# Exponentials left in the scores' PSUM bank, masks built on the chip, first weight blocks converted in halves

## The chip, the cores and the metric

The kernel runs on one core of one Trainium2 chip, in one launch. Its time is the device time in microseconds (us). Each measurement below is the median of several runs, with the lowest and the highest beside it. A separate profiled execution gives the trace: every instruction of the engines TensorE (PE for its products, PEld for its weight loads), VectorE (DVE), ScalarE (ACT), GpSimd (POOL) and SyncE (SP, which only issues DMAs here).

## The reference, cut to what matters

Sliding-window attention feeds a three-matrix mixture layer, and that a SiLU layer:

```
attention: q, k, v of (4, 8, 576, 64); S = q k^T / 8; position i sees j with 0 <= i - j < 64
           x = softmax(masked S) v, heads side by side: (2304, 512)
layer 1:   h = (x w1) * (x w2);  x2 = (h w3) w_out     w1, w2: 512 x 1024, w3: 1024 x 1024, w_out: 1024 x 512
layer 2:   h = x2 w_in;  out = (h * sigmoid(h)) w_out  w_in: 512 x 2048, w_out: 2048 x 512
```

The weights reach the chip as 64-bit floating point words, and the chip makes 32-bit numbers of them.

## The kernel before, in words

**Converting a weight.** Weights come in chunks of 128 x 512 numbers, that is 128 x 1024 32-bit words, 512 KB each, by a DMA of SP's queue. A chunk takes five steps: ACT scales the high words (L125, tile cv_b) and rounds the low words (L128, cv_r), DVE shifts (L138, cv_z) and puts the sign in (L141), and POOL adds the two (L145). The chunks of w1 and w2 then get a rounded half and a rest (L153, L157). `line` is the list of chunks; `loads_to` issues their DMAs, `steps_to` and `fill` drop their steps in between other work.

**Attention.** The 2304 positions are 18 units of 128, with 4 pairs of heads each: 72 groups g. A group has two heads, and each of its steps works for both. The scores (PE, L329 for the first 17 groups, L333 and L337 for the rest) go to the PSUM tile s, 128 x 2 x 192, of which there is one buffer: 128 queries against 192 keys. DVE adds a mask to each head, scales, writes the result to the SBUF tile sm and takes the extreme of each row into nm (L344, two instructions; the masks are constants, tile consts, loaded by three DMAs of SP). ACT raises each head to its exponential in place in sm, with the row's sum in es (L355: each of the two is an ACTIVATE and a READ of the accumulator). DVE adds the parts of the sum (L363), takes the reciprocal (L365) and multiplies (L367, "the normalise", which reads and writes sm). PE transposes the result (L377, three instructions, tile t), ACT and DVE take it out of PSUM (L383, or L387 to L392), and PE multiplies it with the values (L404 to L412, tile o). ACT and DVE take o out (L419 to L422), and POOL finishes it (L423, xr). sm has two buffers, used in turn.

**Stage W, 0 to about 93 us.** Since nothing lies between the products with w3 and with w_out, the chip first computes wp = w3 w_out: 16 steps s of 4 products (L582, 128x512 each), with one chunk of w3 each, and in the first 8 steps one of w_out too. Chunks of w1 and w2 follow among them at the steps that W12_BY names. `half(h)` runs half a group: the even half issues for g, in this order on PE, the scores of g, the values of g-2 and the transposes of g-1, and on ACT the exponentials of g; the odd half issues on DVE the normalise of g, and the preparations of later groups (L297 to L321). 28 halves stand in this stage. Before it, "spin" products on a constant tile (L525) keep PE at work.

**Stage A, 93 to about 401 us.** Six blocks of 384 positions. Each has 24 units of products, one group of the attention to every two: 16 "ab" units (L618: x w1 and x w2, multiplied elementwise over L632, L634 and split by L85) and 8 "x" units (L648, with wp; L601 takes the result out, L602 stores it). The other groups run here.

**Layer 2, to the end.** Products hx, hy (L828) and o (L882), with sums of weights and activations made by ACT, DVE and POOL.

**What sets the order.** Each engine runs its instructions in the order in which the program issues them, and waits at each for the semaphores of what it needs. The order is written out, by the loops above; no scheduler changes it.

## Time and profile before

| | us |
|---|---|
| median of 3 runs (lowest, highest) | 841.4 (841.26, 842.33) |
| the profiled execution | 841.24 |
| its span, from the first to the last instruction | 839.5 |
| busy: PE / PEld / DVE / ACT / POOL | 827.4 / 745.9 / 615.3 / 561.2 / 529.7 |

The span is what the trace shows; 1.74 us of the profiled execution lie outside of it. PE's granted clock is 1.000 of full speed over the whole span. In the rows further down, a row of a timeline tells when an instruction started, how long it took, its engine, line and operation, the tile written and the tile read, and in brackets how long the engine was idle before it and what released it. A row of the groups tells the busy time of all instructions of one line and shape and the mean of one in ns.

### The profile page before, as it was taken

How to read it: one execution, taken by the hardware profiler on the slowest of the kernel's cores; microseconds unless marked ns; L12 is line 12 of the kernel's file. 1: busy time of each engine (PE TensorE's matmuls, PEld its weight loads, DVE VectorE, ACT ScalarE, POOL GpSimd, SP SyncE). 2: the span in 40 equal slices, each digit the busy share in tenths (PEclk: the TensorE clock that was granted, in tenths of full speed). 3: DMA queues.
4: the chain of work that ended last, by engine and by line, in shares of the span. 5: the costliest groups of instructions: out<-in, count | busy, mean ns of one | idle time of the engine just before them, and what ended most of it. 6: DMA issues, size and time to landing. Idle time of an engine off the chain costs nothing.

```text
span 839.5 us, 14173 instructions
## 1 busy us (share of the span) xinstructions
PE 827.4 (99%) x4418; PEld 745.9 (89%) x4418; DVE 615.3 (73%) x1424; ACT 561.2 (67%) x1390; POOL 529.7 (63%) x588
## 2 busy tenths in 40 slices
PE   7999999999999999999999999999999999999998
PEld 3555799999999999999999988888888888988986
DVE  7889877688888888888368698998644567644544
ACT  6889778898898898898556566556543446443433
POOL 5768666677777677677565577876454456454441
PEclk9999999999999999999999999999999999999999
DMA  9998234444544544543433522301301201201002
GB/s 320 330 321 279 72 107 128 149 127 133 167 150 142 169 156 145 170 157 103 155 134 120 194 76 76 125 26 51 102 26 56 95 26 64 88 25 51 1 1 75
DMA packets 54682, 102.66 MB, mean 122 GB/s; under 512 B 5200, under 2 KB 32592, under 8 KB 54608
## 3 DMA queue, kind: packets, MB, share of 16 engines
q1 hardware_dynamic: 51008, 96.91, 35.5%
q10 hardware_dynamic: 3600, 4.85, 1.6%
q8 instruction: 35, 0.57, 0.3%
q14 instruction: 39, 0.32, 0.1%
HBM read 88.11 MB, written 13.63 MB: 121 GB/s over the span
## 4 chain that ended last, share of the span: by engine, by line
PE 69%; POOL 8%; ACT 6%; issue 4%; DVE 1%; ACTq 0%; POOLq 0%; DVEq 0%
PE o L882 24%; PE ab L618 14%; PE hy L828 12%; PE hx L828 9%; PE x L648 6%; POOL klo L303 2%; POOL vhl L321 1%; ACT sm L355 1%; PE t L377 1%; POOL xr L423 1%; ACT qkhi L297 1%; POOL p L88 1%; POOL cv_b L189 1%; PE o L411 1%; PE s L333 1%
## 5 line engine op out<-in xcount | busy, mean ns | idle before, releaser
L882 PE MATMUL o<-hl,gp 128*128 128x512 f32 x504 | 133.3, 394 | 0.0
L618 PE MATMUL ab<-xa,hl 128*128 128x384 f32 x576 | 119.0, 341 | 0.0
L828 PE MATMUL hy<-xop,j 128*128 128x384 f32 x576 | 115.9, 335 | 0.0
L618 PE MATMUL ab<-xb,hl 128*128 128x384 f32 x570 | 115.2, 334 | 0.0
L88 POOL TENSOR_TENSOR gp<-tmp,gp 128x384 fp32r<-128x384 f32 x56 | 64.1, 1145 | 77.5 <-ACT gp L85 75.9
L828 PEld LDWEIGHTS hy<-xop,j 128*128 128x128 f32 x576 | 102.6, 188 | 9.0 <-DVE tmp L722 1.0
L882 PEld LDWEIGHTS o<-hl,gp 128*128 128x128 f32 x504 | 93.1, 188 | 13.1
L618 PEld LDWEIGHTS ab<-xb,hl 128*128 128x128 f32 x570 | 100.3, 188 | 0.0
L618 PEld LDWEIGHTS ab<-xa,hl 128*128 128x128 f32 x576 | 99.1, 188 | 0.0
L844 ACT ACTIVATE tmp<-hx 128x384 f32<-128x384 f32 x48 | 23.6, 492 | 111.5 <-DVE hx L722 67.8
L722 DVE TENSOR_TENSOR tmp<-hy,tmp 128x384 f32<-128x384 f32 x96 | 53.2, 554 | 56.1 <-PE hy L828 51.5
L828 PE MATMUL hx<-xop,j 128*128 128x384 f32 x432 | 86.6, 335 | 0.0
L882 PE MATMUL o<-hl,gq 128*128 128x512 f32 x324 | 85.9, 393 | 0.0
L88 POOL TENSOR_TENSOR gq<-tmp,gq 128x384 fp32r<-128x384 f32 x36 | 39.0, 1084 | 74.3 <-ACT gq L85 74.3
L828 PEld LDWEIGHTS hx<-xop,j 128*128 128x128 f32 x432 | 76.8, 188 | 4.1
L423 POOL TENSOR_TENSOR xr<-ot 128x128 f32<-128x128 f32 x55 | 32.7, 594 | 73.7 <-DVE ot L422 65.5
L303 POOL TENSOR_TENSOR klo<-qk,qkhi 64x192 fp32r<-64x192 f32 x110 | 67.2, 611 | 7.6 <-ACT qkhi L297 2.7
L882 PEld LDWEIGHTS o<-hl,gq 128*128 128x128 f32 x324 | 60.3, 188 | 11.2
L648 PE MATMUL x<-p,wp 128*128 128x384 f32 x360 | 69.6, 339 | 0.0
L355 ACT ACTIVATE sm<-sm,nm 128x192 f32<-128x192 f32 x144 | 64.5, 450 | 3.9 <-DVE nm L344 2.5
L648 PEld LDWEIGHTS x<-p,wp 128*128 128x128 f32 x360 | 61.9, 188 | 0.0
L145 POOL TENSOR_TENSOR cv_b<-cv_b,cv_r 128x512 int32<-128x512 int32 x32 | 48.6, 1520 | 18.8 <-DVE cv_b L141 9.4
(146 smaller groups left out, 1896.7 us busy)
## 6 DMA issues: line engine op xcount, KB each, us to landing
qk<-in_qkv SPq DMA_DIRECT2D x55, 384.0 KB, 3.1
words<-in_w_out SPq DMA_DIRECT2D x24, 512.0 KB, 5.4
r<-w_in SPq DMA_DIRECT2D x22, 512.0 KB, 3.4
words<-in_w3t SPq DMA_DIRECT2D x16, 512.0 KB, 6.5
words<-in_w SPq DMA_DIRECT2D x16, 512.0 KB, 6.2
xe<-in_w_in SPq DMA_DIRECT2D x16, 512.0 KB, 4.8
v<-in_qkv SPq DMA_DIRECT2D x55, 96.0 KB, 2.7
x2d<-x2s ACTq DMA_DIRECT2D x24, 192.0 KB, 1.9
```

The source lines that it names most:

```text
L88: (nc.vector if eng_lo == "dve" else nc.gpsimd).tensor_tensor(out=lo, in0=src, in1=f32(hi), op=ALU.subtract)
L145: nc.gpsimd.tensor_tensor(out=x, in0=b, in1=self.r, op=ALU.add)
L189: nc.gpsimd.tensor_tensor(out=self.b, in0=self.b, in1=self.r, op=ALU.add)
L303: nc.gpsimd.tensor_tensor(out=k_lo[g % 2][hs, h * 192 : h * 192 + 192], in0=t[hs, n], in1=f32(hi[hs, n]), op=ALU.subtract)
L355: nc.scalar.activation(out=x, in_=x, func=AF.Exp, scale=-1.0, bias=nm[:, h : h + 1], accum_out=sums_of[g % 2][:, h, 0:1])
L423: nc.gpsimd.tensor_tensor(out=xr[:, c, r : r + 128], in0=t[:, 0:128], in1=t[:, 128:256], op=ALU.add)
L618: nc.tensor.matmul(acc, lhsT=w[:, l, fs], rhs=x[k // 2][:, k % 2, r, :], start=(k == 0 and n == 0), stop=(k == 3 and n == 2),)
L648: nc.tensor.matmul(acc, lhsT=wp[f][:, l, o * 128 : (o + 1) * 128], rhs=p[f][:, r, :], start=(f == 0 and n == 0), stop=(f == 7 and n == 2),)
L722: eng.tensor_tensor(out=out, in0=a, in1=b, op=op)
L828: nc.tensor.matmul(bank[name], lhsT=w[:, l, at + kt], rhs=x[:, kt, r, :], start=(fresh and kt == 0 and n == 0), stop=(kt == 1 and n == 2), ...
L844: nc.scalar.activation(out=sg, in_=src, func=AF.Sigmoid)
L882: nc.tensor.matmul(oacc[t], lhsT=g[:, l, cols], rhs=weights["out", 2 * p + i][:, r, :], start=(p == 0 and i == 0 and n == 0), stop=(p == P ...
```

## The change

It has five parts. (1) The exponentials write to the scores' PSUM tile instead of sm, and the normalise reads that tile and writes sm. (2) The even half of a group issues on PE the values of g-2, the transposes of g-1 and then the scores of g. (3) The masks and the identity are built in consts by memsets on DVE and selections on POOL, the mask of the rarest kind by a copy and two memsets on POOL at step 4; the three mask DMAs are gone, and the zeroing of kq moves to DVE and that of klo to step 4. (4) The first chunks, 0, 1 and 3, are converted in halves of 256 columns, the first step issues its four products in a row, and SP's first loads have another order. (5) The second chunk of w1 is due at step 4 instead of 3.

On PE in stage W, around the scores of group 8: o6 are the values of group 6, t7 the transposes of group 7, s8 the scores of group 8, accw the products of w3 with w_out. Before:

```order
L329 MATMUL s8_608<-kq0_81 128x384
L404 MATMUL o6_618<-pw0_96,vp0_83 128x128
L405 MATMUL o6_618<-pw0_96,vp0_83 128x128
L406 MATMUL o6_618<-pw0_96,vp0_83 128x64
L377 MATMUL t7_623<-consts_69,sm1_78 128x128 x3
L582 MATMUL accw1_2_589<-wo_94,q_95 128x512
L582 MATMUL accw1_3_590<-wo_94,q_95 128x512
L582 MATMUL accw1_0_587<-wo_94,q_95 128x512
L582 MATMUL accw1_1_588<-wo_94,q_95 128x512
```

With the change:

```order
L451 MATMUL o6_647<-pw0_96,vp0_83 128x128
L452 MATMUL o6_647<-pw0_96,vp0_83 128x128
L453 MATMUL o6_647<-pw0_96,vp0_83 128x64
L424 MATMUL t7_651<-consts_69,sm1_78 128x128 x3
L376 MATMUL s8_655<-kq0_81 128x384
L617 MATMUL accw1_2_628<-wo_94,q_95 128x512
L617 MATMUL accw1_3_629<-wo_94,q_95 128x512
L617 MATMUL accw1_0_626<-wo_94,q_95 128x512
L617 MATMUL accw1_1_627<-wo_94,q_95 128x512
```

The scores s8 move from ahead of o6 and t7 to behind them; the products around them stay.

On ACT in an ab stretch, group 40 or 39: pt are the transposed probabilities, the ACTIVATEs are the exponentials of the two heads, sm0 the SBUF tile, s40 the PSUM tile of the scores, a and ot what follows. In brackets is what an instruction waits for; "Activation" is ACT's own semaphore. Before:

```order
L387 CAST pt3_957<-t39_2985 128x2x128 [waits PE_49,Activation_49]
L389 CAST pt1_955<-t39_2985 64x64 [waits Activation_49] x2
L355 ACTIVATE sm0_77,es0_86<-sm0_77,nm40_2976 128x192 [waits DVE_49,Activation_49] x2
L632 COPY a2_2_3011<-ab2_4_2998 128x384 [waits DMAHW1_49,PE_49]
L419 COPY ot38_3016<-o38_2981 64x256 [waits Pool_49]
L420 COPY ot38_3016<-o38_2981 64x256
```

With the change:

```order
L434 CAST pt3_995<-t39_3014 128x2x128 [waits PE_49]
L436 CAST pt1_993<-t39_3014 64x64 x2
L402 ACTIVATE s40_3018,es0_86<-sm0_77,nm40_3022 128x192 [waits DVE_49,PE_49,Activation_49]
L402 ACTIVATE s40_3018,es0_86<-sm0_77,nm40_3022 128x192 [waits Activation_49]
L702 COPY a2_2_3049<-ab2_4_3036 128x384 [waits DMAHW6_49,PE_49]
L466 COPY ot38_3054<-o38_3010 64x256 [waits Pool_49]
L467 COPY ot38_3054<-o38_3010 64x256
```

Before, the two exponentials have the same kinds of wait, DVE's semaphore for their own mask and ACT's for a value that it reached 18 instructions or more ahead. With the change the first waits for both masks and for PE's scores, and ACT's semaphore at the second is awaited at the value that the first exponential sets.

On PE at the program's start. Before:

```order
L525 MATMUL spin<-idle_in 128x512 x3
L329 MATMUL s_152<-kq_81 128x384
L525 MATMUL spin<-idle_in 128x512
L582 MATMUL accw_0_172<-wo,q 128x512
L582 MATMUL accw_1_173<-wo,q 128x512
L329 MATMUL s_195<-kq_82 128x384
L377 MATMUL t_201<-consts,sm_77 128x128 x3
L582 MATMUL accw_2_174<-wo,q 128x512
L582 MATMUL accw_3_175<-wo,q 128x512
```

With the change:

```order
L573 MATMUL spin<-idle_in 128x512 x3
L376 MATMUL s_176<-kq_81 128x384
L573 MATMUL spin<-idle_in 128x512
L617 MATMUL accw_0_218<-wo,q 128x512
L617 MATMUL accw_1_219<-wo,q 128x512
L617 MATMUL accw_2_220<-wo,q 128x512
L617 MATMUL accw_3_221<-wo,q 128x512
L424 MATMUL t_226<-consts,sm_77 128x128 x3
L376 MATMUL s_230<-kq_82 128x384
```

The first step's four products stand in a row, and the scores of group 1 come behind the transposes of group 0.

The diff, without the host's function for the masks and the kernel's argument for them:

```diff
@@ -29,7 +29,7 @@
 PLAIN = 17
 CVB, CVR = 5, 3
 W12_A, W12_B = 3, 13
-W12_BY = [n * W12_A // 8 for n in range(8)] + [W12_A + n * (W12_B - W12_A) // 8 for n in range(8)]
+W12_BY = [(n - 1) * W12_A // 7 if n > 3 else 0 for n in range(8)] + [W12_A + n * (W12_B - W12_A) // 8 for n in range(8)]
 
 
 def mask_kind(u):
@@ -62,6 +62,34 @@
     consts = att.tile([128, 896], F32, name="consts", tag="mask", bufs=1)
     mask_at = (384, 0, 640)
     id_sb = consts[:, 256:384]
+
+    def select(t, op, base, rows, step, fill):
+        nc.gpsimd.affine_select(
+            out=t, in_=t, compare_op=op, fill=fill, base=base, pattern=[[step, t.shape[1]]], channel_multiplier=rows
+        )
+
+    def build_first():
+        m = consts[:, 0:256]
+        nc.vector.memset(m[:, 0:64], MASKED)
+        nc.vector.memset(m[:, 64:192], 0.0)
+        nc.vector.memset(m[:, 192:256], MASKED)
+        nc.vector.memset(id_sb, 0.0)
+        select(m[:, 64:192], ALU.is_ge, 63, -1, 1, MASKED)
+        select(m[:, 64:192], ALU.is_ge, 0, 1, -1, MASKED)
+        select(id_sb, ALU.not_equal, 0, 1, -1, 1.0)
+
+    def build_band():
+        m = consts[:, 384:640]
+        nc.vector.memset(m, 0.0)
+        select(m[:, 0:192], ALU.is_ge, -1, -1, 1, MASKED)
+        select(m[:, 64:192], ALU.is_ge, 0, 1, -1, MASKED)
+        select(m[:, 192:256], ALU.is_ge, -1, -1, 1, MASKED)
+
+    def build_across():
+        nc.gpsimd.tensor_copy(out=consts[:, 640:896], in_=consts[:, 384:640])
+        nc.gpsimd.memset(consts[64:128, 640:768], MASKED)
+        nc.gpsimd.memset(consts[64:128, 832:896], MASKED)
+
     idle_in = att.tile([128, 512], F32, name="idle_in", tag="pt3", bufs=1)
     for i in range(4):
         nc.vector.memset(idle_in[:, i * 128 : i * 128 + 128], 0.37 * i - 0.73)
@@ -126,6 +154,25 @@
             if part != 0:
                 self.r = slot("cv_r", "cv_r", [512], I32, bufs=CVR)
                 nc.scalar.activation(out=self.r, in_=low.bitcast(U32), func=AF.Copy, scale=2.0**-29)
+
+        def in_halves(self):
+            w = self.words.rearrange("p (n two) -> p n two", two=2)
+            low, high = w[:, :, 0], w[:, :, 1]
+            b = slot("cv_b", "cv_b", [512], I32, bufs=CVB)
+            r = slot("cv_r", "cv_r", [512], I32, bufs=CVR)
+            z = converting["z"]()
+            self.begun = True
+            for n in (slice(0, 256), slice(256, 512)):
+                nc.scalar.activation(out=f32(b[:, n]), in_=f32(high[:, n]), func=AF.Copy, scale=2.0**-112)
+                nc.scalar.activation(out=r[:, n], in_=low[:, n].bitcast(U32), func=AF.Copy, scale=2.0**-29)
+                nc.vector.tensor_scalar(
+                    out=z[:, n], in0=b[:, n], scalar1=3, scalar2=None, op0=ALU.logical_shift_left
+                )
+                nc.vector.scalar_tensor_tensor(
+                    out=b[:, n], in0=high[:, n], scalar=-0x80000000, in1=z[:, n],
+                    op0=ALU.bitwise_and, op1=ALU.bitwise_or,
+                )
+                nc.gpsimd.tensor_tensor(out=self.out.bitcast(I32)[:, n], in0=b[:, n], in1=r[:, n], op=ALU.add)
 
         def stage1(self):
 
@@ -346,25 +393,25 @@
                 op0=ALU.add, op1=ALU.min, scale=-(D ** -0.5), scalar=3.0e38, accum_out=nm[:, h : h + 1],
             )
         fill()
-        s_st[g] = (nm, rs)
+        s_st[g] = (nm, rs, s_ps)
 
     def exps(g):
-        nm, rs = s_st[g]
+        nm, rs, e = s_st[g]
         for h in range(2):
             x = sm[g % 2][:, h, :]
             nc.scalar.activation(
-                out=x, in_=x, func=AF.Exp, scale=-1.0, bias=nm[:, h : h + 1], accum_out=sums_of[g % 2][:, h, 0:1]
+                out=e[:, h, :], in_=x, func=AF.Exp, scale=-1.0, bias=nm[:, h : h + 1], accum_out=sums_of[g % 2][:, h, 0:1]
             )
 
     def normalise(g):
-        _, rs = s_st.pop(g)
+        _, rs, e = s_st.pop(g)
         x = sm[g % 2]
         fill()
         nc.vector.tensor_reduce(out=rs, in_=sums_of[g % 2], axis=mybir.AxisListType.X, op=ALU.add)
         fill()
         nc.vector.reciprocal(out=rs, in_=rs)
         fill()
-        nc.vector.tensor_tensor(out=x, in0=x, in1=rs.unsqueeze(2).to_broadcast([128, 2, 192]), op=ALU.mult)
+        nc.vector.tensor_tensor(out=x, in0=e, in1=rs.unsqueeze(2).to_broadcast([128, 2, 192]), op=ALU.mult)
 
     def transposes(g):
 
@@ -430,15 +477,16 @@
 
         g, odd = divmod(h, 2)
         if not odd:
+            if 2 <= g <= NG + 1:
+                sums.append(values(g - 2))
+            t_ps = transposes(g - 1) if 1 <= g <= NG else None
             if g < NG:
                 scores(g)
             squeeze(unit_of[0])
-            if 2 <= g <= NG + 1:
-                sums.append(values(g - 2))
-                if plain(g - 2):
-                    sums.pop()()
-            if 1 <= g <= NG:
-                split_t(g - 1, transposes(g - 1))
+            if sums and plain(g - 2):
+                sums.pop()()
+            if t_ps:
+                split_t(g - 1, t_ps)
             if g < NG:
                 exps(g)
         else:
@@ -528,48 +576,73 @@
 
         for t in kq:
             for h, hs in HEADS:
-                nc.gpsimd.memset(t[hs, 320 - h * 320 : 512 - h * 320], 0.0)
-        for t in k_lo:
-            for h, hs in HEADS:
-                nc.gpsimd.memset(f32(t)[hs, 192 - h * 192 : 384 - h * 192], 0.0)
+                nc.vector.memset(t[hs, 320 - h * 320 : 512 - h * 320], 0.0)
+        build_first()
+        build_band()
         spin(3)
         loads_to(2)
         load_qk(0)
-        nc.sync.dma_start(out=consts[:, 0:384], in_=mask[:, 0:384])
         loads_to(4)
         load_qk(1)
-        nc.sync.dma_start(out=consts[:, 384:640], in_=mask[:, 384:640])
         loads_to(6)
+        def begin(c, between):
+            c.stage0(0)
+            between()
+            c.stage0(1)
+            for f in c.stage1():
+                f()
+            c.begun = True
+
+        t_ps = None
+
+        def second():
+            split_t(0, t_ps)
+            exps(1)
+
+        line[0].in_halves()
+        line[1].in_halves()
+        scores(0)
+        load_qk(2)
         load_v(0)
-        load_v(1)
-        load_v(2)
-        steps_to(2)
-        for f in line[1].stage1():
-            f()
-        scores(0)
         spin(1)
-        line[2].stage0(0)
-        exps(0)
-        line[2].stage0(1)
-        for f in line[2].stage1():
-            f()
-        for x in line[1:3]:
-            x.begun = True
-        done["step"] = 3
-        halves[0] = 1
+        begin(line[2], lambda: exps(0))
+        loads_to(8)
+        half(1)
+        line[3].in_halves()
+        done["step"] = 5
+        halves[0] = 3
         acc, split_done = {}, set()
+
+        def product(s, j, i):
+            nc.tensor.matmul(
+                acc[i], lhsT=w3x[s % 7][:, i * 128 : (i + 1) * 128], rhs=wo[:, j], start=(j == 0), stop=(j == 7)
+            )
+
         for s in range(16):
             sw, j = divmod(s, 8)
             loads_to(ready[s + 2] + (3 if s > 5 else 1 if s > 1 else 0))
-            if s == 9:
-                nc.sync.dma_start(out=consts[:, 640:896], in_=mask[:, 640:896])
+            if s == 4:
+                build_across()
+                for t in k_lo:
+                    for h, hs in HEADS:
+                        nc.gpsimd.memset(f32(t)[hs, 192 - h * 192 : 384 - h * 192], 0.0)
             if j == 0:
                 for i in range(4):
                     acc[i] = accumulator(f"accw{sw}_{i}", [128, 512])
             for part in range(2):
                 first = ready[s + 1 if s else 0]
                 steps = first + (ready[s + 2] - first) * (part + 1) // 2
-                if s:
+                if s == 0 and part == 0:
+                    steps = 0
+                elif s == 0:
+                    for i in (2, 3):
+                        product(s, j, i)
+                    t_ps = transposes(0)
+                    scores(1)
+                    begin(line[4], second)
+                elif s == 1 and part == 0:
+                    fill(3)
+                else:
                     steps_to(steps, (nc.vector, nc.gpsimd), 3)
                 halves_to(min(W_HALVES, 2 + W_HALVES * (2 * s + part + 1) // 32))
                 steps_to(steps, (nc.vector, nc.gpsimd), 3)
@@ -578,11 +651,8 @@
                         split_done.add((0, c))
                         split_x(0, c)
                 fill(3)
-                for i in (0, 1) if part == 0 else (2, 3):
-                    nc.tensor.matmul(
-                        acc[i], lhsT=w3x[s % 7][:, i * 128 : (i + 1) * 128], rhs=wo[:, j],
-                        start=(j == 0), stop=(j == 7),
-                    )
+                for i in (0, 1) if part == 0 else (2, 3) if s else ():
+                    product(s, j, i)
                     if j == 7:
                         n = sw * 4 + i
                         wp[n] = slot(f"wp{n}", f"w{16 + n}", [2, 512], F32R)
```

## Rows read from the trace of the kernel before

**Rows 1.** The profile page, part 1: busy time, share of the span, instructions, by engine
```profile
PE 827.4 (99%) x4418; PEld 745.9 (89%) x4418; DVE 615.3 (73%) x1424; ACT 561.2 (67%) x1390; POOL 529.7 (63%) x588
```

**Rows 2.** Timeline of PE, first 20 us: start, duration, engine, line, operation, idle before
```profile
7.61 1.02 PE L525 MATMUL spin<-idle_in 128*128 128x512 f32 x2
9.64 1.98 PE L582 MATMUL accw<-wo,q 128*128 128x512 f32 x4 [1.01 <-POOL q L145]
```

**Rows 3.** Timeline of ACT, first 22 us
```profile
6.05 0.67 ACT L125 ACTIVATE cv_b<-words 128x512 f32<-128x512 f32 x1 [0.42 <-DMA words<-in_w3t]
```

**Rows 4.** Timeline of POOL, first 22 us
```profile
6.70 1.27 POOL L145 TENSOR_TENSOR wo<-cv_b,cv_r 128x512 int32<-128x512 int32 x1 [3.67 <-DVE cv_b L141]
8.32 1.27 POOL L145 TENSOR_TENSOR q<-cv_b,cv_r 128x512 int32<-128x512 int32 x1 [0.35 <-DVE cv_b L141]
```

**Rows 5.** Groups by line and shape, ACT and POOL: busy us, mean ns, idle before
```profile
L780 ACT CAST j<-r 128x256 fp32r<-128x256 f32 x22 | 8.8, 402 | 0.0
L844 ACT ACTIVATE tmp<-tmp 128x384 f32<-128x384 f32 x48 | 25.2, 525 | 21.6 <-DVE tmp L722 21.2
L844 ACT ACTIVATE tmp<-hx 128x384 f32<-128x384 f32 x48 | 23.6, 492 | 111.5 <-DVE hx L722 67.8 <-PE hx L828 43.7
...
L722 POOL TENSOR_TENSOR r_xr<-r_xr 128x256 f32<-128x256 f32 x4 | 3.1, 786 | 1.6 <-DVE j L722 1.4
```

**Rows 6.** Timeline of DVE around group 8 of the attention
```profile
58.03 0.35 DVE L344 CUSTOM_DVE_ANT_0 sm<-s,consts 128x192 f32<-128x192 f32 x1
59.44 0.16 DVE L363 TENSOR_REDUCE rs<-es 128x2 f32<-128x4 f32 x1 [0.17 <-ACT sm L355]
```

**Rows 7.** Timeline of ACT around group 8
```profile
58.43 0.45 ACT L355 ACTIVATE sm<-sm,nm 128x192 f32<-128x192 f32 x1 [1.51 <-DVE nm L344]
```

**Rows 8.** Timeline of PE around group 8
```profile
58.79 0.86 PE L329 MATMUL s<-kq 128*128 128x384 f32 x2
61.05 0.52 PE L377 MATMUL t<-consts,sm 128*128 128x128 f32 x3 [0.79 <-ACT cv_r L128]
```

**Rows 9.** Timeline of ACT, an ab stretch: the exponentials of group 39
```profile
228.74 0.46 ACT L355 ACTIVATE sm<-sm,nm 128x192 f32<-128x192 f32 x1
229.10 0.19 ACT L355 ACTIVATION_READ_ACCUMULATOR sm<-sm,nm 128x1 f32 x1
229.19 0.44 ACT L355 ACTIVATE sm<-sm,nm 128x192 f32<-128x192 f32 x1
```

**Rows 10.** Timeline of ACT: a copy, and the DMA that it is the input of
```profile
270.89 0.48 ACT L601 COPY x2s<-x 128x384 f32<-128x384 f32 x1
271.40 0.33 ACTq L602 DMA_DIRECT2D x2d<-x2s  x1
```

**Rows 11.** Timeline of ACT: the first exponential of groups 27 and 70
```profile
164.22 0.46 ACT L355 ACTIVATE sm<-sm,nm 128x192 f32<-128x192 f32 x1
...
393.87 0.46 ACT L355 ACTIVATE sm<-sm,nm 128x192 f32<-128x192 f32 x1
```

**Rows 12.** Timeline of DVE: the normalise of groups 27 and 70
```profile
165.63 0.56 DVE L367 TENSOR_TENSOR sm<-sm,rs 128x384 f32<-128x384 f32 x1
...
395.28 0.56 DVE L367 TENSOR_TENSOR sm<-sm,rs 128x384 f32<-128x384 f32 x1
```

**Rows 13.** Timeline of PE: two scores, 12 groups apart; the transposes of groups 27, 70
```profile
146.45 0.36 PE L333 MATMUL s<-qkhi 128*128 128x192 f32 x2
...
168.16 0.49 PE L377 MATMUL t<-consts,sm 128*128 128x128 f32 x3
...
209.37 0.36 PE L333 MATMUL s<-qkhi 128*128 128x192 f32 x2
...
395.98 0.52 PE L377 MATMUL t<-consts,sm 128*128 128x128 f32 x3
```

**Rows 14.** Timeline of DVE: a normalise in an x stretch
```profile
282.71 1.36 DVE L367 TENSOR_TENSOR sm<-sm,rs 128x384 f32<-128x384 f32 x1
```

**Rows 15.** Timeline of ACT: the cast of xb after it
```profile
285.65 0.52 ACT L85 CAST xb<-xr 128x384 fp32r<-128x384 f32 x1 [1.61 <-POOL xr L423]
```

More of the change, by code (lines that the diff above doesn't have):

```diff
@@ L42, in tile_window_attention_ffn @@
 @with_exitstack
-def tile_window_attention_ffn(ctx, tc, qkv, qkp, vp, mask, w1, w2, w3t, w_out, w_in, w_out2, out):
+def tile_window_attention_ffn(ctx, tc, qkv, qkp, vp, w1, w2, w3t, w_out, w_in, w_out2, out):
     nc = tc.nc
@@ L1096, in plain_values @@
     return v
-def masks():
-    r = np.arange(128)[:, None]
-    c = np.arange(192)[None, :]
-    band = (c >= r + 1) & (c <= r + WIN)
-    first = band & (c >= 64)
-    across = band & ((r < 64) | (c >= 128))
-    m = np.where(np.stack([band, first, across], 1), 0.0, MASKED)
-    m = np.concatenate([m, m[:, :, 0:64]], 2)
-    return np.concatenate([m[:, 1], np.eye(128), m[:, 0], m[:, 2]], 1).astype(np.float32)
 def kernel(**inputs):
@@ L1119 @@
         "vp": plain_values(qkv),
-        "mask": masks(),
         "w1": inputs["moe_w1"],
```

## The prediction

> **What bounds the kernel now.** I read the busy times first: PE's products fill 99% of the span, with their weight loads (PEld) beside them, and no other engine is busy for more than 73% [rows 1]. So a change pays in two ways only: it takes work from PE, which this one does not (the same products run, in another order), or it takes away the little time in which PE stands still. Then the waits of PE, which lie at two kinds of place. At the start the first product waits for the conversion of the second chunk [rows 2]. Later a few transposes wait for their group's normalise, as in group 8 [rows 6 to 8]. Last I compared the pace of the attention's loop on ACT and DVE with PE's. In stage A the exponentials of group 27 start at 164.22 and those of group 70 at 393.87 [rows 11]: 229.65 us for 43 groups, 5.34 a group. PE needs 62.92 for 12 groups where nothing holds it [rows 13], 5.24 a group, 225.46 for 43. So the loop of the side engines is the slower of the two. It lives on a lead: in group 27 the normalise ends at 166.19 [rows 12] and the transposes start at 168.16 [rows 13], a lead of 1.97; in group 70 it ends at 395.84 and they start at 395.98, a lead of .14, which is a hand-over and no lead at all. The reader is to see in these four rows that the lead is just used up where the attention ends. Whatever makes that loop slower by x a group is paid by PE some 43 times; whatever makes it faster is worth little, since PE is at its own pace.
>
> **The exponentials.** They keep their number. In the present trace the second of a pair starts .45 after the first [rows 9]: its ACTIVATE overlaps the first one's READ, which ends at .36 + .19 = .55. With the change the second waits for the first by ACT's own semaphore. How long such a wait takes no row of this pair shows. The nearest is the copy x2s and the DMA that ACT issues once it is done: .03 after its end [rows 10]. If the first exponential counts as done with the READ, the second starts at .55 + .03 = .58, less what a semaphore instruction fewer may save: +.12. If it is done with its ACTIVATE (.46), the second starts at .49: +.04. What a write to PSUM costs on ACT no row shows; an ACTIVATE that reads PSUM is .033 shorter than one that reads SBUF (492 against 525 ns [rows 5]); if a write gains as much in both, the pair ends .06 earlier. The bounds of the pair are then -.02 and +.12, and I take +.10, next to the upper one, because the READ belongs to the same instruction.
>
> The Trainium skill ("ScalarE: Activation LUTs", section "Step-by-step: what each stage is for") states that PSUM is the faster destination for ScalarE. No run here shows it yet; it speaks for the lower bound, and gives no number.
>
> **The normalise** reads PSUM and SBUF instead of SBUF twice. Alone it takes .56 [rows 12], and I cost it the same. But in an x stretch one took 1.36 [rows 14], while POOL was adding; behind it POOL's xr came late, and ACT's cast of xb waited 1.61 [rows 15]. I take it that the second SBUF operand is the cause, and that with PSUM in its place the normalise takes .56 there too: -.80 for the loop, once in each of three blocks between groups 27 and 70: -2.40. This row is one of the three. If the cause is another, 0.
>
> **The scores behind the transposes.** Where PE has no wait, the order costs nothing. Where the transposes wait for a normalise, the scores formerly ran ahead of the wait and now come after it. In stage A two of their three instructions take .36, overlapped [rows 13], and I take .39 for all, an estimate; in stage W they take .86 with the end that overlaps the next work [rows 8], and I take .65.
>
> **Sum for stage A.** Normalise 70 moves by 43 x .10 for the pairs, +.10 for its own pair, -2.40 for the contention: +2.00. The transposes of group 70 already waited for it, so they move as much, and the scores of group 71 behind them add .39: +2.39. Behind the last group nothing gives this back, since layer 2 runs at PE's pace.
>
> **The start.** Before, the first product starts at 9.64, 1.01 after PE's last spin [rows 2], when POOL has added the second chunk (8.32 + 1.27 = 9.59 [rows 4]). ACT begins that chunk at 6.05, when it has landed [rows 3]. On 256 columns an ACT step takes .40 and a POOL add .79 [rows 5]; a DVE step I put at .40 too, an estimate. A half is then added some .40 + .40 + .40 + .79 = 1.99 after ACT starts on it, 8.04, or with .05 for each of three hand-overs some 8.2. PE is with its spin until 7.61 + 1.02 = 8.63, so the first product comes at about 8.6: -1.0. The mask DMAs (459 KB) also leave their time in the queue to the later chunks; but DVE has the same conversions to do, with more instructions, and holds the next ones back. I carry -.9 to 48 us.
>
> **Stage W behind it.** Group 8's masks start at 58.03, the first exponential follows at 58.43 behind the first mask [rows 7], and the reduction at 59.44, 1.41 after the masks [rows 6]. With the change the first exponential waits for both masks, some .28 longer, an estimate (a mask takes .35 [rows 6], and the second overlaps the end of the first), and the pair takes .10 to .12 more: the reduction starts some .40 later. The transposes of that group wait on PE already (61.05, idle .79 [rows 8]), and the scores, formerly in front of them, now come after: .65. Together +1.05. For the stage's later groups I take +.45, an estimate: less than half of group 8's, for fewer of them wait. Stage W thus gives -.9 + 1.05 + .45 = +.6.
>
> **Masks, identity, memsets.** They run on DVE and POOL ahead of the first chunk, in time in which both only wait for it, and cost nothing; what it costs if that cover is gone is the third rival. Zeroing klo moves to step 4, in POOL's idle time. A chunk of w1 is converted one of sixteen steps later, and stage A, which reads it, comes after the last of them: 0.
>
> **Total.** +2.39 + .6 = +3.0. The profiled execution took 841.24, .16 below the median of the runs; 841.24 + 3.0 = **844.2**.
>
> **Rivals.** (A) Faster: the pair costs nothing, because ACT is done with the ACTIVATE alone and PSUM takes the result sooner. For it: the row of the ACTIVATE that reads PSUM [rows 5]. Against it: the READ that stands behind every exponential [rows 9]. By the sums above the total is .6 + .39 - 2.40 + 44 p for a cost p of the pair, that is -1.4 + 44 p, down to PE's own pace (225.46 - 227.82 = -2.4, 227.82 being the time between the two transposes [rows 13], + .6 = -1.8). At p = -.02 that is 839.5; from p below -.01 on it is faster by a measurable amount. The Trainium skill ("ScalarE: Activation LUTs", the sentence above) would lead here.
>
> (B) No difference: p between 0 and .07, or the wait costs .10 and contention gives back more than I count, since every normalise might be disturbed a little. -1.4 + 44 x .05 = +.8: 842.0. For it: ACT has idle moments that could swallow a part. Against it: the one that I know [rows 15] is a part of the same loop.
>
> (C) Slower at the start: POOL's selections are late, and all additions queue behind them. Before its first addition POOL is idle for 3.67 us [rows 4], and within them it may have got ready for a kind of instruction that it had not yet run; the trace shows no more than that this took 3.67 or less, hidden. With the change that lies in front of six selections, from about .7 us on, which is when the program begins. A selection has 128x192 elements at most and so should take no more than the add's .79 [rows 5], 4.7 in all; half of that at the least. They end between 3.1 and 9.1, and three half additions (2.4) must follow before the first product: 8.6, as in the forecast, up to 11.5, +2.9. Weighted to the late end, C is +2.3 on the forecast: 846.5. It decides once the selections end after 6.2.
>
> The Trainium skill ("GPSIMD Engine Reference", section "2.1 Instruction dispatch") states some 6 us for the first call to freshly loaded code. By it rival C would pass its upper end. Before the first addition the trace has 3.67 us of idle time [rows 4], less than the page says.
>
> **How the numbers follow.** Forecast (p from .07 to .12: 843 to 845.1) .53; A .18; B .20; C .09. A measurement of this kernel tells about 0.2%, 1.7 us, from no change, so faster is below 839.7 and slower above 843.1. A is faster in nearly all of its cases, and a part of B, in which the start keeps its whole gain, too: .20. Slower: the forecast without its lowest cases, and C: .55. The rest, .25, is the same. The range for 8 in 10 begins at 839.6, A's place, of which the lower half is left out, and ends at 846.5, the middle of C.
>
> **What would show it.** Right: the second exponential starts .55 to .58 after the first, in every group; 43 groups from group 27 on take about 231.6 to 232 on ACT; the transposes of many more groups in stage A wait for their normalise; the normalise takes .56 throughout; the first product is at about 8.6. Wrong: pairs still .45 to .49 apart, or a shorter ACTIVATE that pays for the wait; then A or B holds. If the first product comes after 9.64 with POOL's selections before it, C. If the 1.36 of a normalise stays although it reads PSUM, the contention was not with its second operand, and the time is above 846.

## The result: slower by 1.1%, and where the time went

The changed kernel takes 851.0 us (median of 4 runs, 849.96 to 852.0), the kernel before 841.87 in the same comparison (4 runs, 841.26 to 842.44). The ratio is 1.0108, with a 95% interval of 1.0092 to 1.0124. The forecast was slower, 844.2; two thirds of the loss were not in it.

The profiled execution has a span of 850.2, 10.7 more than before's 839.5. Its first part, which answers to [rows 1], shows that PE did not get more work, but is busy 6.7 us longer and stands still for the rest:

```profile
PE 834.1 (98%) x4418; PEld 748.6 (88%) x4418; DVE 604.1 (71%) x1439; ACT 569.1 (67%) x1396; POOL 523.3 (62%) x596
```

Where the loss comes in is read from PE's timeline at the places that were shown of before (start, duration, line, operation, idle time before and its releaser):

```profile
8.97 3.70 PE L617 MATMUL accw<-wo,q 128*128 128x512 f32 x8 [0.25 <-POOL q L175]
...
19.28 0.52 PE L424 MATMUL t<-consts,sm 128*128 128x128 f32 x3 [3.14 <-DVE sm L414]
...
64.55 0.62 PE L424 MATMUL t<-consts,sm 128*128 128x128 f32 x3 [2.21 <-DVE sm L414]
64.96 1.49 PE L376 MATMUL s<-kq 128*128 128x384 f32 x2
...
85.21 0.79 PE L424 MATMUL t<-consts,sm 128*128 128x128 f32 x3 [1.98 <-DVE sm L414]
...
176.83 0.49 PE L424 MATMUL t<-consts,sm 128*128 128x128 f32 x3
...
406.37 0.52 PE L424 MATMUL t<-consts,sm 128*128 128x128 f32 x3 [0.17 <-DVE sm L414]
406.65 0.45 PE L380 MATMUL s<-qkhi 128*128 128x192 f32 x2
```

The first product starts .67 earlier than in [rows 2]. The transposes of group 8 are already 3.50 late against [rows 8], those of group 27 8.67 and those of group 70 10.39 against [rows 13]. So stage W, with what follows it up to group 17 (where the lag is 8.64), loses 8.6, and stage A 2.1 with the scores of group 71, which now come last. The row of the scores at 64.96 shows the second surprise: 1.49 for what took .86 before [rows 8]. The windows of two us around it have PE's granted clock in the column before the DMA share (the first two columns are the window and its length, then come the busy times of PE, PEld, DVE, ACT and POOL, each with its number of instructions):

```profile
60.00:62.00 2.00, 2.00 (x9) 1.04 (x8) 1.91 (x7) 0.22 (x1) 2.00 (x2) 1.00 1.04 381
62.00:64.00 2.00, 0.34 (x4) 0.20 (x2) 1.32 (x5) 1.97 (x7) 1.48 (x3) 1.00 1.04 293
64.00:66.00 2.00, 1.45 (x5) 1.12 (x6) 1.69 (x3) 2.00 (x5) 2.00 (x2) 0.71 0.78 303
66.00:68.00 2.00, 2.00 (x4) 0.72 (x3) 1.25 (x5) 0.87 (x4) 1.62 (x2) 0.50 0.22 73
68.00:70.00 2.00, 2.00 (x6) 1.04 (x5) 1.58 (x5) 2.00 (x6) 0.67 (x1) 0.94 0.76 198
```

PE is busy for .34 us of the window 62 to 64, after which the clock stands at .50, the lower of its two levels (1.2 of 2.4 GHz), until it comes back at 68 to 70. That happens three times in the profiled execution, each time with a wait of 2 to 3 us in front of a group's transposes (groups 1, 8 and 11: the rows at 19.28, 64.55 and 85.21). In the profiled execution before, the granted clock is 1.00 throughout.

The rest of the lag is read from DVE. Its waits in the first 95 us, of the changed kernel and then of the kernel before (what waits, for what, us in total, times, longest):

```profile
DVE sm L391 <- PE s L376: 6.3, 8, 1.4
DVE rs L410 <- ACT s L402: 3.9, 6, 0.7
```

```profile
DVE rs L363 <- ACT sm L355: 2.5, 5, 1.0
```

The first row has no counterpart before: DVE stands eight times at the masks (L391) until PE has made the scores. The second evens out over the first 110 us, which hold all of stage W in both: the reductions wait 4.1 here and 3.9 before. All of DVE's waits listed there make 19.6, against 14.1 before; those for converted chunks (cv_z) got shorter, 3.3 instead of 5.1. ACT waits for the masks in its turn (first 110 us, this kernel, then before):

```profile
ACT s L402 <- DVE nm L391: 15.1, 14, 1.9
```

```profile
ACT sm L355 <- DVE nm L344: 2.5, 3, 1.5
```

In stage A the parts behave much as the forecast had them. ACT's two exponentials of a pair, in an ab stretch:

```profile
253.87 0.42 ACT L402 ACTIVATE s<-sm,nm 128x192 f32<-128x192 f32 x1
254.30 0.20 ACT L402 ACTIVATION_READ_ACCUMULATOR s<-sm,nm 128x1 f32 x1
254.53 0.43 ACT L402 ACTIVATE s<-sm,nm 128x192 f32<-128x192 f32 x1
```

The second starts .66 after the first, instead of .45 [rows 9]; it is .58 to .59 in groups 0 to 17 and about .67 in all others. The ACTIVATE itself became shorter, and the normalise is never disturbed (groups by line and shape: busy us, mean ns):

```profile
L402 ACT ACTIVATE s<-sm,nm 128x192 f32<-128x192 f32 x144 | 61.0, 424 | 18.6 <-DVE nm L391 15.8
```

```profile
L414 DVE TENSOR_TENSOR sm<-s,rs 128x384 f32<-128x384 f32 x72 | 40.1, 557 | 2.5
```

Before, the same two had means of 450 and 729 ns. The Trainium skill ("ScalarE: Activation LUTs", section "Step-by-step: what each stage is for") calls PSUM the faster destination for ScalarE, and this trace agrees, by 26 ns; the wait between the two costs more than that gives.

### The profile page after: what moved, and what is told of

Same layout as the page of the kernel before. It is cut to its first block, busy times and chain, and to the rows that moved or that the text cites. A ratio compares the mean times of both kernels' runs of the same rounds, so it can differ in the third digit from the quotient of the medians.

```text
span 850.2 us, 13905 instructions
## 1 busy us (share of the span) xinstructions
PE 834.1 (98%) x4418; PEld 748.6 (88%) x4418; DVE 604.1 (71%) x1439; ACT 569.1 (67%) x1396; POOL 523.3 (62%) x596
## 4 chain that ended last, share of the span: by engine, by line
PE 62%; ACT 19%; DVE 7%; issue 4%; ACTq 0%; POOL 0%; DVEq 0%
PE o L952 24%; PE hy L898 12%; PE hx L898 9%; PE ab L688 8%; ACT s L402 5%; PE x L718 5%; DVE a L704 2%; ACT pt L436 2%; PE accw L617 2%; DVE ot L469 2%; ACT ot L467 2%; ACT a L702 2%; ACT ot L466 1%; ACT p L113 1%; ACT qkhi L344 1%
## 5 line engine op out<-in xcount | busy, mean ns | idle before, releaser
L688 PE MATMUL ab<-xa,hl 128*128 128x384 f32 x576 | 116.5, 336 | 0.0
L688 PEld LDWEIGHTS ab<-xa,hl 128*128 128x128 f32 x576 | 101.7, 188 | 0.8
L402 ACT ACTIVATE s<-sm,nm 128x192 f32<-128x192 f32 x144 | 61.0, 424 | 18.6 <-DVE nm L391 15.8
```

What stands on the lines that cost most here:

```text
L402: nc.scalar.activation(out=e[:, h, :], in_=x, func=AF.Exp, scale=-1.0, bias=nm[:, h : h + 1], accum_out=sums_of[g % 2][:, h, 0:1])
L688: nc.tensor.matmul(acc, lhsT=w[:, l, fs], rhs=x[k // 2][:, k % 2, r, :], start=(k == 0 and n == 0), stop=(k == 3 and n == 2),)
```

## The experiments

In the order in which they answer. Beside each time stands the time of the kernel before in the same comparison. "The lag at group 17" is how much later than before its transposes start in the profiled execution; two pairs of runs whose stage W is the same program differ in it by .66 (stage A alone and the version that beats both, below) and by .83 (the pair apart, 9.47, and the changed kernel, 8.64), so less than that says nothing.

**The start alone.** The changed kernel with the attention's part of the kernel before.

```diff
-            if 2 <= g <= NG + 1:
-                sums.append(values(g - 2))
-            t_ps = transposes(g - 1) if 1 <= g <= NG else None
             if g < NG:
                 scores(g)
...
-                out=e[:, h, :], in_=x, func=AF.Exp, ...
+                out=x, in_=x, func=AF.Exp, ...
-        nc.vector.tensor_tensor(out=x, in0=e, in1=rs...
+        nc.vector.tensor_tensor(out=x, in0=x, in1=rs...
```

> The start alone: masks on the chip, halves, four products in a row and the later chunk of w1 as in the changed kernel, but the attention as before (exponentials in SBUF, scores ahead of values and transposes). Theory 1 (the attention's part lost the time: scores behind the transposes and a serial pair of exponentials, and PE's clock fell in the waits that they made): 839.5 to 841.5, no stretch of lower clock. Rival (the new start, with its order of loads and conversions, lost it in stage W): 846 to 850.

Measured: 841.57 (before 841.28), ratio 1.0002, 0.9993 to 1.0012. The rival is out: the new start loses nothing. It gains nothing either, though a stretch of lower clock was there against the expectation, at 18 to 24, behind a wait of 2.7.

**The attention's part alone**, on the kernel before, with the same lines the other way round.

> The attention's part alone on the kernel before: exponentials in the scores' bank, values, transposes, scores in this order; masks, first chunks and w1 as before. Theory 1: about 850, with waits of PE above 2 us and stretches of lower clock in stage W. Rival (the new start): 843 to 844, the pair's 1.6 us in stage A and little else.

Measured: 851.0 (one run, so without an interval; before 841.28). This part alone makes as much as the whole loss.

**Only the new order on PE.** The changed kernel, with exponentials and normalise in SBUF (the last four lines of the first diff).

> The changed kernel with the exponentials and the normalise back in SBUF, so that of the attention's part only the new order on PE is left. If the order makes most of stage W's loss: 846 to 848, stage A at the old pace (no 1.6 us), DVE still waiting for the scores some 6 us in the first 95. If the exponentials in PSUM make it: 841 to 843, and few waits of DVE for the scores.

Measured: 845.82 (before 841.28), ratio 1.005, 1.0034 to 1.0066. Between the two expectations: the order is about half of the loss, the exponentials the other. DVE waits 5.0 for the scores in the first 95 us; one long stretch of lower clock at 18 to 26.

**The clock.** PE's long waits are filled with products that nobody reads, in the bank of the transposes that follow.

```diff
         t_ps = psa.tile([128, 384], F32, name=f"t{g}", tag="t")
+        for _ in range({1: 7, 4: 2, 8: 5, 11: 4}.get(g, 0)):
+            nc.tensor.matmul(t_ps, lhsT=idle_in[:, 0:128], rhs=idle_in[:, 0:384], start=True, stop=True)
```

> The changed kernel with extra products of 128x384, whose result nobody reads, in front of the transposes of groups 1 (seven), 4 (two), 8 (five) and 11 (four), that is in PE's long waits. If the granted clock falls because PE stands still there: clock 1.000 throughout, and 4 to 5 us less than the changed kernel, 846 to 847. If the lower clock has another cause or costs nothing in the end: 850 to 852, since the extra products take no other engine's time.

Measured: 849.15 (two runs; before 841.28), ratio 1.0094, 1.0074 to 1.0115. That is 7.87 above the kernel before, where the changed kernel is 9.13 above it: 1.3 less (1.85 by the bare medians), for more work on PE. The two intervals overlap, so these times alone do not settle the size. The changed kernel's own four runs point the same way: two with a mean granted clock of .994 took 852.0 and 851.86, two with .996 took 850.15 and 849.96. So do the three runs of the order alone (846.08 and 845.82 at .996, 844.29 at .998). The profiled execution of the changed kernel is the one of 852.0, so its profile shows the lower clock's share at its largest. In the profiles the lag at group 17 falls from 8.64 to 6.02, and the windows that had .34 of work and then half the clock now read:

```profile
62.00:64.00 2.00, 2.00 (x8) 1.21 (x7) 1.61 (x5) 2.00 (x6) 1.47 (x2) 1.00 0.89 268
64.00:66.00 2.00, 2.00 (x10) 1.29 (x9) 1.12 (x2) 1.70 (x4) 2.00 (x3) 1.00 0.60 240
66.00:68.00 2.00, 2.00 (x7) 0.80 (x6) 1.30 (x6) 1.18 (x5) 1.05 (x1) 1.00 0.22 65
```

So the clock falls because PE stands still, and this costs some 1.3 to 2.6 us, less than the 4 to 5 expected. That the next wait would have taken a part of it anyway is my reading, not shown.

**Start and order without the clock's part.** The same fillers in front of the transposes of group 1, five in the start alone, seven in the order alone.

```diff
+        for _ in range({1: 5}.get(g, 0)):      the start alone
+        for _ in range({1: 7}.get(g, 0)):      the order alone
```

> The new start alone (attention as in the kernel before) with five extra products of 128x384 in front of the transposes of group 1, where PE stood still for 2.7 us and the granted clock fell behind it. If the lower clock hid a gain of the new start: clock 1.000, and about 1.2 to 1.6 less than without the extra products, 839.9 to 840.5. If the start has no gain: 841.3 to 841.8.

Measured: 841.86 (before 841.81), ratio 1.0003, 0.9994 to 1.0012, clock 1.000. The lower clock hid no gain of the start.

> The changed kernel with the exponentials and the normalise in SBUF (only the new order is left of the attention's part) and seven extra products of 128x384 in front of the transposes of group 1. It takes the lower clock out of the order's cost: clock 1.000; if DVE's waits for the scores make most of that cost, 843 to 844.5; if the clock did, 841.5 to 842.5.

Measured: 844.2 (before 841.81), ratio 1.0031, 1.0021 to 1.0041, clock 1.000. The order alone had 4.5 with the lower clock in it and has 2.4 without: the second pair of runs in which the clock's share shows, and the same way, though the two ratios' intervals overlap a little (1.0034 to 1.0066, 1.0021 to 1.0041). DVE's waits in this run, first 95 us:

```profile
DVE sm L391 <- PE s L376: 3.1, 4, 1.3
DVE rs L410 <- ACT sm L402: 1.0, 6, 0.2
```

**The start's halves.** The start alone, with chunks 0, 1 and 3 whole.

```diff
-            for n in (slice(0, 256), slice(256, 512)):
+            for n in (slice(0, 512),):
```

> The new start alone (attention as before), but chunks 0, 1 and 3 converted whole. If the halves, which need more time of DVE and POOL, ate the start's gain: the groups of stage W come .5 to 1 earlier than in the start with halves, and the time is 840.5 to 841.3. If something else in the start did (order of loads, four products in a row): 841.5 to 842.5.

Measured: 841.74 (before 841.68), ratio 1.0001. The time is that of the second case. Without halves the groups of stage W come .57 later, not .5 to 1 earlier, and .57 is within what runs differ, so the halves did not eat the gain. What did is not shown. To read there is this: from 10 to 43.5 us DVE is busy for 30.93 of 33.5 in the start alone, and for 30.39 before (third pair of columns behind PE and PEld):

```profile
10.00:43.50 33.50, 30.10 (x103) 16.24 (x101) 30.93 (x72) 27.78 (x67) 23.52 (x25) 0.95 1.02 330
```

```profile
10.00:43.50 33.50, 30.29 (x108) 16.07 (x107) 30.39 (x75) 27.75 (x66) 22.78 (x17) 1.00 0.98 334
```

DVE has little room there, so a product that comes earlier can hardly move its conversions forward. But PE is as busy (30.10 and 30.29), and no run tested which of the two holds the other.

**Stage A alone.** The kernel before, with exponentials in the bank and the new order from group 18 on.

```diff
+LATE = 18
...
-                out=x, in_=x, func=AF.Exp, ...
+                out=e[:, h, :] if g >= LATE else x, in_=x, func=AF.Exp, ...
```

> The kernel before, with exponentials in the scores' bank and the new order on PE from group 18 on; start and stage W as before. It shows what the attention's part costs in stage A by itself. If the pair's wait is its cost: 843 to 844, the loop at 5.42, the groups up to 17 as before, and no waits of PE in stage A that reach 1 us. If most of stage A's loss in the changed kernel came from its late arrival there: 841 to 842.

Measured: 843.94 (before 841.68), ratio 1.0025, 1.0014 to 1.0037. The lag grows from .50 at group 17 to 2.5 at the end: stage A alone costs 2.0 (2.3 by the times), near the forecast's 2.4, and does not need the late arrival.

**The pair apart.** In the changed kernel, ACT takes the transposed tile out between the two exponentials, from group 18 on.

```diff
-            if t_ps:
+            if g < NG and t_ps and not plain(g - 1):
+                exps(g, (0,))
                 split_t(g - 1, t_ps)
-            if g < NG:
-                exps(g)
+                exps(g, (1,))
...
```

> The changed kernel, but in the split groups (17 and later) ACT takes the transposed tile out of PSUM between the two exponentials of a pair instead of ahead of them, so that the second has not to wait for the first. If the pair's wait is what makes stage A 1.7 slower: the loop goes from 5.42 to about 5.30 a group, stage A takes some 2 to 2.5 us less than in the changed kernel, 848.5 to 849.5. If the pair's wait is hidden, or the late transposed tile costs as much: 850.5 to 852.

Measured: 859.87 (before 841.81), ratio 1.0214. Wrong, and by much. ACT in an ab stretch of that run, from the cast of p to the copy of a:

```profile
240.31 0.52 ACT L113 CAST p<-a 128x384 fp32r<-128x384 f32 x1 [0.28 <-DVE a L709]
240.95 0.43 ACT L402 ACTIVATE s<-sm,nm 128x192 f32<-128x192 f32 x1
...
241.40 0.35 ACT L434 CAST pt<-t 128x256 fp32r<-128x256 f32 x1
...
241.98 0.42 ACT L402 ACTIVATE s<-sm,nm 128x192 f32<-128x192 f32 x1
...
242.64 0.48 ACT L707 COPY a<-ab 128x384 f32<-128x384 f32 x1
```

From 240.31 to 242.64 it is 2.33; in the changed kernel, with the pair together, it is 2.24 (252.86 to 255.10). The first exponential, moved forward, now starts right behind the cast, and there its mask is not always ready:

```profile
ACT s L402 <- DVE nm L391: 7.1, 8, 1.7
```

(That is stage A, 113 to 421 us.) In stage A of the changed kernel the exponentials wait for the masks .8 us in all. DVE, too, now waits for ACT's copy of the transposed tile (L437, for pt of L436) 54 times, 48.9 us in all, where the changed kernel has 18 such waits and 13.6 us; which of the two waits brings the other about is not shown. So the pair's wait could not be hidden in this place; whether it can in another was not tried. The same pair apart, in the start alone with five fillers, from group 18 on, with the exponentials in the bank and the new order on PE from there too:

```diff
+            if g < NG and apart:
+                exps(g, (0,))
             if t_ps:
                 split_t(g - 1, t_ps)
             if g < NG:
-                exps(g)
+                exps(g, (1,) if apart else (0, 1))
```

> A version that should beat both: the new start with the five extra products, the attention as before in stage W, and from group 18 on the exponentials in the scores' bank, the new order on PE, and the two exponentials of a pair apart. If the pair's wait is the only cost of the new form in stage A, and the undisturbed normalise its gain: stage A at PE's pace, 1 to 2 us less than the kernel before there, 838 to 839.5. If the new form costs in stage A by the order too: 841 to 843.

Measured: 851.51 (before 841.81), ratio 1.0116. The same two waits are there in stage A (113 to 421 us): the exponentials wait 8.0 for their masks, and DVE 50.9 for pt. The lag is .34 at group 17, .30 at group 20, and grows from there to 10.3 at the last group.

**A version that beats both.** The kernel before, with the new order on PE from group 18 on, exponentials in SBUF.

```diff
-            if g < NG:
+            late = g >= LATE
+            if g < NG and not late:
+                scores(g)
+            if late and 2 <= g <= NG + 1:
+                sums.append(values(g - 2))
+            t_ps = transposes(g - 1) if late and g <= NG else None
+            if g < NG and late:
                 scores(g)
...
```

> The kernel before, with only the order values, transposes, scores on PE, and that only from group 18 on; start, masks and exponentials as before. In the changed order with exponentials in SBUF, stage A was 1.1 shorter than before's. If that is the order's own gain: 840.0 to 841.0, about 1 less than the kernel before. If it came from the later start of that run: 841.2 to 842.

Measured: 840.6 (11 runs; before 841.68, 25 runs), ratio 0.9988, 0.9979 to 0.9997. Small, but outside of no change. Two normalises that POOL disturbed are now free of it in a block (this kernel, then the kernel before, which has three in this block; the last is [rows 14]):

```profile
277.41 0.60 DVE L368 TENSOR_TENSOR sm<-sm,rs 128x384 f32<-128x384 f32 x1
...
282.61 0.64 DVE L368 TENSOR_TENSOR sm<-sm,rs 128x384 f32<-128x384 f32 x1
```

```profile
271.58 1.40 DVE L367 TENSOR_TENSOR sm<-sm,rs 128x384 f32<-128x384 f32 x1
...
277.51 1.64 DVE L367 TENSOR_TENSOR sm<-sm,rs 128x384 f32<-128x384 f32 x1
```

They start within .1 of where they did, and take .60 and .64 instead of 1.64 and 1.36. POOL's additions beside them did move: that of cv_b starts .15 behind the first normalise (277.56) instead of .07 ahead of it (277.44), and that of xb at 281.83 instead of 282.64. Two are free of it in the next block too, none in the block before. That the gain in time comes from them is not shown.

## Why the prediction was wrong, step by step

The comparisons make a ladder, each against the kernel before on its own chip: start +0.05 to +0.3; with the order +2.4, so 2.1 to 2.3 for it; with the exponentials in PSUM +7.9 (fillers in place), so 5.5 for them; with the clock free to fall +9.1, so 1.3 for it (2.6 by the lag of the profiled execution).

- **The start: right in its place, wrong in what it carries.** The first product was forecast at 8.6 and comes at 8.97 [rows 2]. I carried -.9 to 48 us; the start alone ends at no gain. The forecast itself named a likely reason (DVE has the same conversions to do), but counted it as a tenth of the gain instead of all of it.
- **Stage W behind the start: this step failed.** It said +.6 in total, and 8.6 came. The failed term is "the scores, formerly in front of them, now come after: .65", taken once where PE waits. It counted the order on PE's side only. DVE runs in order too, and the masks of a group stand in its queue ahead of the conversions: with the scores behind the transposes, DVE waits at the masks (6.3 us in the first 95, none before; 3.1 with the order alone and the clock at 1.00). The wait then goes round: ACT's exponentials wait for the masks, DVE's normalise for the exponentials, PE's transposes for the normalise (9.2 us at five of them in the first 110; before, its transposes waited 3.8 at four, 2.2 of it for normalises), and the next scores stand behind these. By the lag at group 17 without the clock's part (6.02 with fillers, 3.54 with the order alone, 1.05 for the start alone) order and exponentials cost 2.5 each, to within the .66 to .83 by which equal stages differ; with 1.05 for the start and 2.6 for the clock they make up the 8.64. That the order and the exponentials cost this much is shown by runs; the way round is read from the waits, and no run took one of them away by itself. Nor is DVE alone what stage W goes by: in the chain that ended last, ACT's exponentials and conversions fill the time from 74.3 to 82.9, between a group's masks and a normalise.
- **The exponentials' part of it** was right in kind and in size in the one group that it was worked out for. In group 8 the reduction starts 1.89 after the masks, where 1.41 + .40 = 1.81 was forecast [rows 6]:

```profile
61.05 0.35 DVE L391 CUSTOM_DVE_ANT_0 sm<-s,consts 128x192 f32<-128x192 f32 x1
...
62.94 0.16 DVE L410 TENSOR_REDUCE rs<-es 128x2 f32<-128x4 f32 x1 [0.65 <-ACT s L402]
...
63.85 0.56 DVE L414 TENSOR_TENSOR sm<-s,rs 128x384 f32<-128x384 f32 x1
```

  But I had it in group 8 and a flat .45 for the rest, and I take it that this .48 belongs to every group of stage W, since each group's scores now wait for the normalise of the group before. (That each group pays is argued from the order of the queues; the runs show the sum, and do not tell the pair's wait from the bank that stays taken until the normalise.)
- **The clock was not in the forecast at all.** It had seen only rows at 1.000 and did not ask what longer waits would do.
- **Stage A: right in its sum, in part by luck.** Forecast +2.39; the lag grows from 8.64 at group 17 to 10.7 at the end, and by 2.0 in the run that has stage A's part alone. From the cast of p to the copy of a, ACT takes 2.24 where it took 2.15 (232.94 to 235.09 before): .09 for the pair, .10 was forecast. The pair itself grew by more than that: from the first start to the end of the second READ it takes 1.22 (253.87 to 255.09) instead of .99 (234.08 to 235.07), though each ACTIVATE is .026 shorter; what makes up for it is that the first exponential starts .59 behind the start of the cast of pt instead of .73. The first exponentials of groups 27 and 70,

```profile
173.26 0.43 ACT L402 ACTIVATE s<-sm,nm 128x192 f32<-128x192 f32 x1
...
404.03 0.42 ACT L402 ACTIVATE s<-sm,nm 128x192 f32<-128x192 f32 x1
```

  are 230.77 apart, 1.12 more than before [rows 11], where 2.00 was forecast and 231.6 to 232 was to show it right; the lead at group 27 is 1.37 instead of 1.97 [rows 12, 13], a loss of .60 that the sum left out. With the .39 of the scores that is 2.11. The two errors nearly cancel. One cause of the first is a misread count: the forecast took one disturbed normalise in each of three blocks, -2.40. Before, there are three in each block, nine between groups 27 and 70, of 1.31 to 1.64 each, and none is left: 8.1 us of DVE's time, of which the loop got back some 2.8 (43 x .09 less 1.12). The normalise is .56 throughout, as forecast [rows 12, 14].
- **Rivals.** A falls with the .58 to .68 and the .09 that the pair costs ACT. So does B's first form; its second (contention gives back more than counted) is borne out in kind by the nine normalises, but it did not give back what the pairs cost, and stage W decided. C falls with POOL's timeline: the six selections are done at 4.68, and the first addition waits for ACT, not for them:

```profile
2.94 1.74 POOL L67 TENSOR_SCALAR_AFFINE_SELECT consts<-consts 128x128 f32<-128x128 f32 x6 [2.50 <-DVE consts L74]
6.22 0.73 POOL L175 TENSOR_TENSOR wo<-cv_b,cv_r 128x256 int32<-128x256 int32 x1 [1.54 <-ACT cv_r L167]
```

## What to carry to other kernels

When work is moved behind a wait on one engine, look at every engine that takes its result in order: the wait can appear there once per turn, and go round to the first engine. Two exponentials of ACT into one PSUM tile were put one behind the other by a semaphore here, .58 to .68 apart instead of .45; that is cheap once, and dear on a loop that has no lead. Ask of every new wait of TensorE how long it is: those of 2 to 3 us here were paid a second time, in a clock of .50 after them.

## What was not expected of the hardware

The clock's fall to .50 with a wait of 2 to 3 us, and its return only in the window 68 to 70, though PE is busy again from 64.55 on. Extra products that nobody reads, in these waits, kept the clock at 1.00 and took some 1.3 us off, as the profiles and the clocks of the single runs bear out, with intervals that overlap. And that the same normalise takes .56 with PSUM as its source in all 72 groups, where with SBUF it took up to 1.64 beside POOL's work.
